# Fused windowed attention, Fourier mixing and a two-layer network on one core: more query and key buffers, a first load in three pieces, and PSUM banks lent to the first two batches

## The chip, the core and the metric

The kernel runs on one core of a Trainium2 chip. Its engines run side by side and are tied together by semaphores: TensorE (PE; its weight loads are shown apart as PEld), VectorE (DVE), ScalarE (ACT), GpSimd (POOL) and SyncE (SP). SP does nothing here but issue DMA transfers; ACT and POOL issue a few. The metric is the device time of one execution in microseconds, median of the runs.

## What is computed

All data is float32. Attention first: 8 batches, 8 heads, 576 positions, 64 columns a head. Heads 0 to 3 look at the last 32 positions, heads 4 to 7 at every fourth of the last 128. Its output, 576 rows of 512 a batch, goes through a Fourier mixing, a normalisation and two matrix products of 512 x 2048 and 2048 x 512:

```python
scores = np.where(masks, (q @ k.T) / sqrt(64), -1e9)
attn = exp(scores - max);  attn /= attn.sum() + 1e-9
x = (attn @ v)                       # (8, 576, 512)
u = x + real(fft(fft(x, axis=1), axis=2))
un = (u - mean(u)) / sqrt(var(u) + 1e-6)
out = u + relu(un @ w_ch1) @ w_ch2
```

## The kernel before

**A planner writes the order.** The program is not written in the order in which it runs. Each piece of work is given to a planner (`add`) with its engine, an estimated cost, the buffers it reads and writes, and a priority (the lower, the sooner). At build time the planner walks through an assumed clock: whenever an engine is free it takes the piece of lowest priority whose inputs are done and whose buffer has come free. A transfer is held back while eight of its queue are under way. The result is one fixed list for each engine, and on the chip each engine takes its list in order. `PAD_*` and `LAND` are lags added to the planner's costs, and the `P_*` constants are the priorities, in units of one attention step (twelve steps, 0 to 11, make a batch; batch b starts at 12 b).

**Attention.** A batch has four pairs of heads (`dil` 0 or 1, `j` 0 or 1). `attend_pair` loads a pair's keys into kb (L523, two transfers of 64 partitions), its queries into tq (L525) and its values into vt (L526), and calls `attend` three times (u = 0, 1, 2), each for two blocks of 96 queries. One such unit is: scores into a PSUM bank sc (L540), add the mask and take the maximum on VectorE into pm and mx (L548), exponential on ScalarE (L554), four transposes into bank pt (L567), a copy to ptsb on ScalarE (L570), the products with vt into bank av (L574), and on VectorE sums, reciprocal and the scaled result xt (L582 to L586). There are two tq buffers and three kb buffers. Keys are kept with zero halves around them, which `start` clears once with memsets (L478, L479). `store` writes xt to DRAM (xsp and xsm, L621).

**PSUM.** Eight banks in all: two each for sc, mix and ff, one each for pt and av.

**Mixing.** `mix` loads a batch's rows again (L693, L702; priority `P_FD` ahead of the work), folds them on POOL and VectorE, multiplies by the sequence and channel tables (L756, L802, banks mix), and normalises. The tables are loaded on POOL's queue by `table` (L499).

**Weights and fills.** The two weight matrices come as 64-bit numbers and are turned into float32 pairs by `words_of` and `halves` (L881 load, L882 on ScalarE, L884 to L893 and L900 on VectorE). `prep_w` does this for the first five of the sixteen blocks of 128 hidden columns, with priority `P_W + P_WF * f`; these stay on the core. `fill` computes the part of the two products that these five blocks give, 256 tokens at a time (L953 up, bank ff, L961 the split of h on VectorE, L969 down), with priority `P_FILL + 4 b P_FILLT` for batch b. There are 18 fills, and they need no more than the five blocks and the tokens, so the planner puts them where PE has room.

**The second half.** When all batches are mixed, the other eleven blocks are prepared, and nine chunks of 512 tokens run through them: five times `two_tiles`, once `one_tile`, with the down products of the tile before (`lower`) put between their up products (L1230). PE does almost nothing else from about 500 us on.

Of the kernel before, what the change touches and what calls it, by code (L numbers as in the profile page):

```python
# [19 lines left out]
P = 128  # L20
# [6 lines left out]
NX = 4  # L27
NKB = 3
NV = 4
NTQ = 2  # L30
NUT = 4
NUC = 2
NH = 6
NLATE = 4
NPE = 1
LO1 = 'DVE'
P_QK0, P_V0 = -7.8, -7.0
P_ST, P_FD, P_WD, P_ST0, P_FD0, P_SPAN0, P_SPAN1 = -4.0, -21.87, -10.91, 0.0, 0.0, 23.02, 23.31
P_QK, P_V, P_TR, P_MIX, P_SPAN, P_W, P_WF, P_FILL, P_FILLT = -8.0, -5.77, -5.0, 3.69, 13.04, 15.31, 8.7, 44.08, 3.7
P_MIX0, P_MIX1 = 3.0, 2.27  # L40
T_SEQ, T_CHN, T_STEP, P_SEQ, P_CHN = 7.07, 19.07, 0.08, -17.52, -2.0
PAD_PE, PAD_DVE, PAD_ACT, PAD_POOL, LAND = 0.0, 0.0, 0.0, 0.0, 1.5
XB = 1
P_MASK, P_ID, P_PERM = -7.19, -5.28, -7.0
NCH = B * S // TOK
# [336 lines left out]
def fused_kernel(ctx: ExitStack, tc, q, k, v, w1, w2, seq, tail, chn, alt, mask, ident, perm, flip, out):  # L382
# [76 lines left out]
    def dma(fn, r, w, prio, nbytes, slow=1):  # L459
        return add("SP", 0.46, fn, r, w, prio, nbytes * slow)  # L460
# [53 lines left out]
    def attend_pair(b, dil, j, xts, when):  # L514
        lead = when(0) + (P_QK if b else P_QK0)
        first = b == 0 and dil == 0 and j == 0
        tq = attw("tq", [P, S], F32, NTQ)
        kb = kbs[(4 * b + 2 * dil + j) % NKB]
        vt = attw("vt", [P, 2, S // QB, D + 1], F32, NV)
        on, eng = (nc.scalar, "ACT") if first else (nc.sync, "SP")  # L520
        for e in range(2):
            ps = slice(64 * e, 64 * e + 64)
            add(eng, 0.5, lambda e=e, ps=ps: on.dma_start(out=kb()[ps, e, WIN:], in_=k[b, dil, j, ps]),  # L523
                (), ((kb, e),), lead, 64 * S * 4)
        dma(lambda: nc.sync.dma_start(out=tq(), in_=q[b, dil, j]), (), (tq,), lead, P * S * 4)  # L525
        dma(lambda: nc.sync.dma_start(out=vt(), in_=v[b, dil, j]), (), (vt,), when(0) + (P_V if b else P_V0),  # L526
            P * 2 * (S // QB) * (D + 1) * 4)
        for u in range(3):
            attend(b, dil, j, u, tq, kb, vt, xts[u], when(u))

    def attend(b, dil, j, u, tq, kb, vt, xt, prio):
        blocks = (u, u + 3) if dil else (2 * u, 2 * u + 1)
        masks = DIL_MASK if dil else PLAIN_MASK
        sc = bank("sc")
        for n, t in enumerate(blocks):
            cols = slice(QB * t, QB * t + QB)
            keys = slice(QB * t, QB * t + KB)

            def scores(n=n, cols=cols, keys=keys):
                nc.tensor.matmul(  # L540
                    sc()[:QB, 256 * n:256 * n + 256], lhsT=tq()[:, cols], rhs=kb()[:, :, keys], start=True, stop=True,
                )
            add("PE", pe4(256), scores, (tq, kb), ((sc, n),), prio)
        pm = attw("pm", [QB, 4, KB], F32, 3)
# [8 lines left out]
        for i in range(4):  # L553
            add("ACT", 0.295, lambda i=i: nc.scalar.activation(  # L554
                out=pm()[:, i], in_=pm()[:, i], func=AF.Exp, bias=mx()[:, i:i + 1], scale=-1.0),
                ((mx, i),), ((pm, i),), prio)
        ps = bank("pt")
        for i in range(4):
# [12 lines left out]
            out=pt().rearrange("p i q -> p (i q)"), in_=ps()[:, :4 * QB]), (ps,), (pt,), prio)  # L571
        av = bank("av")
        for i in range(4):
# [716 lines left out]
    def one_tile(p, lower):  # L1290
        w = ups[p]
        z = bank("ff")
        product(z, 0, [(w[0], 0), (w[1], 1)], True, True, (z, 0))
        h1 = put_h(lambda: z()[:, 0:TOK1], ((z, 0),), False)
        lower(2)
        product(z, TOK1, [(w[2], 2), (w[0], 5)], True, True, (z, 1))
        h2 = put_h(lambda: z()[:, TOK1:TOK], ((z, 1),), False)
        lower(8)
        return [((h1, h2), downs[2 * p])]
# [46 lines left out]
```

## Time and profile before

| | us |
|---|---|
| median of 3 runs | 1099.94 (1099.26 to 1101.09) |
| the profiled execution, its own time | 1098.52 |
| its span in the trace | 1096.7 |
| PE busy | 1059.4 (97%) |
| VectorE busy | 742.9 (68%) |
| ScalarE busy | 520.9 (47%) |
| POOL busy | 283.1 (26%) |

The profiled execution's time is 1.8 us more than its span, which begins and ends with the core's own work. A busy PE is one that has matmuls under way, at whatever clock; the granted clock stands in a column of its own.

### The profile page before, as it was taken

The page shows a single profiled execution, that of the slowest core. Times are in us where ns is not written, and L with a number is a line of the kernel's source. Part 1 is how long each engine was busy: PE and PEld are TensorE (multiplying, and loading weights), DVE is VectorE, ACT ScalarE, POOL GpSimd, SP SyncE. Part 2 cuts the span into 40 slices and gives each one's busy share as a digit, 9 for nine tenths or more (in the row PEclk, how much of TensorE's full clock was granted, in tenths as well). Part 3 has the DMA queues.
Part 4 walks back from the last instruction along what each step waited for, and adds up shares of the span by engine and source line. Part 5 has one row for each costly group of instructions (what it writes and reads, how often), then busy time and mean ns, then how long its engine had stood idle before and what let it go on. Part 6 is the DMA issues. An engine that isn't in the chain of part 4 may idle for free.

```text
span 1096.7 us, 20233 instructions
## 1 busy us (share of the span) xinstructions
PE 1059.4 (97%) x7066; PEld 938.5 (86%) x7066; DVE 742.9 (68%) x2335; ACT 520.9 (47%) x1331; POOL 283.1 (26%) x334
## 2 busy tenths in 40 slices
PE   5889999999999998999999999999999999999998
PEld 4568889888888887899998988989899989898987
DVE  6689978878676759866899864637464555555432
ACT  4688845565465543424465434333333333333431
POOL 2023453544433415330000421212122130312200
PEclk9889999999999999999999999999999999999999
DMA  9687845756464533435634341404050505040211
GB/s 294 198 250 212 247 132 170 211 140 198 144 186 133 139 107 100 113 105 156 173 120 134 102 108 39 115 27 129 1 154 1 154 1 154 1 122 32 91 65 39
DMA packets 104310, 137.05 MB, mean 125 GB/s; under 512 B 9656, under 2 KB 62328, under 8 KB 104208
## 3 DMA queue, kind: packets, MB, share of 16 engines
q1 hardware_dynamic: 100624, 126.85, 41.0%
q0 software_dynamic: 3040, 8.09, 2.3%
q8 instruction: 56, 0.92, 0.4%
q10 hardware_dynamic: 544, 0.82, 0.2%
q14 instruction: 46, 0.38, 0.1%
HBM read 97.92 MB, written 37.80 MB: 124 GB/s over the span
## 4 chain that ended last, share of the span: by engine, by line
PE 80%; DVE 11%; DMA 3%; ACT 2%; issue 2%; SPq 1%; POOL 0%; ACTq 0%; DVEq 0%; POOLq 0%
PE sc L969 14%; PE ff L1230 12%; PE mix L1230 7%; PE sc L540 7%; PE ff L953 7%; PE ff L969 6%; PE av L969 5%; PE pt L969 5%; PE av L574 5%; PE mix L756 3%; PE mix L802 3%; PE pt L567 3%; PE pt L953 2%; DMA ut<-us 2%; DVE pm L548 2%
## 5 line engine op out<-in xcount | busy, mean ns | idle before, releaser
L554 ACT ACTIVATE pm<-pm,mx 96x128 f32<-96x128 f32 x384 | 129.6, 394 | 47.3 <-DVE mx L548 44.1
L540 PE MATMUL sc<-kb,tq 128*96 128x256 f32 x384 | 110.7, 405 | 10.9 <-DMA kb<-in_k_dram 6.9
L1246 ACT COPY s<-ff 128x256 f32<-128x256 f32 x135 | 50.1, 371 | 144.4 <-PE ff L1230 143.8
L548 DVE CUSTOM_DVE_ANT_0 pm<-sc,mask_sb 96x128 f32<-96x128 f32 x384 | 92.3, 280 | 31.5 <-PE sc L540 29.3
L953 PE MATMUL ff<-ut,wa 128*128 128x256 f32 x780 | 106.8, 287 | 4.2 <-DVE h L961 3.9
L969 PE MATMUL sc<-wa,h 128*128 128x512 f32 x420 | 104.4, 391 | 0.0
L953 PEld LDWEIGHTS ff<-ut,wa 128*128 128x128 f32 x780 | 97.1, 189 | 6.6 <-DVE h L961 4.7
L1098 POOL TENSOR_TENSOR ut<-ut 128x512 f32<-128x512 f32 x32 | 49.5, 1566 | 186.1 <-DVE ut L1051 185.5
L574 PEld LDWEIGHTS av<-vt,ptsb 128*96 128x96 f32 x768 | 77.1, 167 | 21.3 <-ACT ptsb L570 8.9
L969 PE MATMUL ff<-wa,h 128*128 128x512 f32 x390 | 93.9, 392 | 0.3 <-DVE r L645 0.3
L574 PE MATMUL av<-vt,ptsb 128*96 128x65 f32 x768 | 82.1, 249 | 8.8 <-ACT ptsb L570 4.4
L969 PEld LDWEIGHTS sc<-wa,h 128*128 128x128 f32 x420 | 76.0, 188 | 13.8
L1051 DVE STREAM_TRANSPOSE ut<-ut 128x512 f32<-128x512 f32 (+1 forms) x76 | 72.2, 982 | 18.7 <-DMA ut<-us 18.5
L969 PE MATMUL sc<-wd,h 128*128 128x512 f32 x324 | 84.1, 393 | 0.0
L969 PEld LDWEIGHTS ff<-wa,h 128*128 128x128 f32 x390 | 71.3, 188 | 14.4 <-DVE r L645 0.5
L1277 DVE TENSOR_TENSOR c<-s,s 128x256 f32<-128x256 f32 x45 | 26.7, 594 | 77.5 <-ACT s L1246 77.5
L1230 PEld LDWEIGHTS ff<-xb,pair 128*128 128x128 f32 x540 | 73.7, 188 | 6.0 <-ACT s L1246 0.3
L540 PEld LDWEIGHTS sc<-kb,tq 128*96 128x96 f32 x384 | 57.9, 173 | 24.0 <-issue 6.8
L1230 PE MATMUL ff<-xb,pair 128*128 128x256 f32 x540 | 76.4, 280 | 0.0
L1251 ACT ACTIVATE h<-row 128x256 fp32r<-128x256 f32 x90 | 37.6, 417 | 65.4 <-DVE row L1284 35.7
L1230 PE MATMUL mix<-xb,pair 128*128 128x256 f32 x486 | 65.1, 278 | 0.8 <-DVE row L1284 0.8
L969 PEld LDWEIGHTS sc<-wd,h 128*128 128x128 f32 x324 | 56.9, 188 | 9.6 <-DVE h L1253 0.3
(163 smaller groups left out, 2248.6 us busy)
## 6 DMA issues: line engine op xcount, KB each, us to landing
vt<-in_v_dram SPq DMA_DIRECT2D x32, 390.0 KB
ut<-in_w_dram SPq DMA_DIRECT2D x20, 512.0 KB
us<-uc SPq DMA_DIRECT2D x36, 257.0 KB
tq<-in_q_dram SPq DMA_DIRECT2D x32, 288.0 KB
part<-row SPq DMA_DIRECT2D x36, 256.0 KB
ut<-us SPq DMA_DIRECT2D x36, 256.0 KB
ut<-part SPq DMA_DIRECT2D x36, 256.0 KB
kb<-in_k_dram SPq DMA_DIRECT2D x62, 144.0 KB
```

The source lines that it names most:

```text
L540: nc.tensor.matmul(sc()[:QB, 256 * n:256 * n + 256], lhsT=tq()[:, cols], rhs=kb()[:, :, keys], start=True, stop=True,)
L548: nc.vector.tensor_tensor_reduce(pm()[:, i], sc()[:QB, KB * i:KB * i + KB], mask_sb()[:, masks[blocks[i // 2]]], -0.125, 3.0e38, ALU.add, ...
L554: add("ACT", 0.295, lambda i=i: nc.scalar.activation(out=pm()[:, i], in_=pm()[:, i], func=AF.Exp, bias=mx()[:, i:i + 1], scale=-1.0), ((mx ...
L567: nc.tensor.transpose(ps()[:, QB * i:QB * i + QB], pm()[:, i], order)
L574: add("PE", 0.17, lambda i=i: nc.tensor.matmul(av()[:QB, 65 * i:65 * i + 65], lhsT=pt()[:, i], rhs=vt()[:, i % 2, blocks[i // 2]], start=T ...
L953: nc.tensor.matmul(z()[:, :n_tok], lhsT=wf()[:, a, kk], rhs=ut()[:, p, kk], start=(kk == 0 and n == 0), stop=(kk == KT - 1 and n == 2),)
L969: nc.tensor.matmul(acc(), lhsT=h()[:, a, P * s:P * s + P], rhs=wf()[:, p], start=(first and n == 0), stop=(last and n == 2),)
L1051: nc.vector.transpose(out=o[back], in_=x[:, g])
L1098: add(name, cost(C), lambda: engine.tensor_tensor(out=made(i)(), in0=x(), in1=y(), op=ALU.subtract), (*done, *((raw, ("s", j)) for j in af ...
L1230: nc.tensor.matmul(z()[:, lo:lo + TOK1], lhsT=ap()[:, a, kk], rhs=xb()[:, j, p, kk], start=(start and k == 0), stop=(stop and k == 6 * len ...
L1246: add("ACT", act(TOK1), lambda: nc.scalar.copy(out=s(), in_=src()[:, :TOK1]), (src,), (s,), SOON - 1)
L1251: add("ACT", act(TOK1), lambda: nc.scalar.activation(out=h()[:, 0], in_=z(), func=AF.Relu), need, ((h, 0),), SOON)
```

## The change

A third tq buffer and a fourth kb buffer. The first pair's k and q are loaded in three pieces of 192 columns, one for each unit: of k only the first piece still goes out on ACT's queue, the rest on SP's, and each unit waits for its own pieces alone. In the first batch every second unit puts its transposes in a mix bank and its products in an ff bank instead of pt and av; in the second batch every second unit puts both in ff banks. `one_tile` takes two ff banks in place of two halves of one. The space reserved for the descriptors of POOL's transfers becomes 8192 bytes a partition. And the planner's priorities and lags get other values: among them, the weights of the first five blocks are due later (`P_W` from 15.31 to 30), fold loads less far ahead of their work (`P_FD` from -21.87 to -10.4), fills spread more (`P_FILLT` from 3.7 to 4.92), and ident_sb sooner (`P_ID`).

```diff
--- before.py
+++ after.py
@@ -25,23 +25,24 @@
 TOK = 4 * P
 TOK1 = 2 * P
 NX = 4
-NKB = 3
+NKB = 4
 NV = 4
-NTQ = 2
+NTQ = 3
 NUT = 4
 NUC = 2
 NH = 6
 NLATE = 4
+NOPEN = 2
 NPE = 1
 LO1 = 'DVE'
 P_QK0, P_V0 = -7.8, -7.0
-P_ST, P_FD, P_WD, P_ST0, P_FD0, P_SPAN0, P_SPAN1 = -4.0, -21.87, -10.91, 0.0, 0.0, 23.02, 23.31
-P_QK, P_V, P_TR, P_MIX, P_SPAN, P_W, P_WF, P_FILL, P_FILLT = -8.0, -5.77, -5.0, 3.69, 13.04, 15.31, 8.7, 44.08, 3.7
-P_MIX0, P_MIX1 = 3.0, 2.27
-T_SEQ, T_CHN, T_STEP, P_SEQ, P_CHN = 7.07, 19.07, 0.08, -17.52, -2.0
-PAD_PE, PAD_DVE, PAD_ACT, PAD_POOL, LAND = 0.0, 0.0, 0.0, 0.0, 1.5
+P_ST, P_FD, P_WD, P_ST0, P_FD0, P_SPAN0, P_SPAN1 = -4.0, -10.4, -10.91, -3.44, -4.94, 29.11, 21.73
+P_QK, P_V, P_TR, P_MIX, P_SPAN, P_W, P_WF, P_FILL, P_FILLT = -8.0, -5.91, -5.0, -1.75, 9.95, 30, 8.7, 42.98, 4.92
+P_MIX0, P_MIX1 = 4.1, 2.27
+T_SEQ, T_CHN, T_STEP, P_SEQ, P_CHN = 7.07, 23.47, 0.08, -5.61, -2.0
+PAD_PE, PAD_DVE, PAD_ACT, PAD_POOL, LAND = 0.0, 0.2, 0.1, 0.2, 1.5
 XB = 1
-P_MASK, P_ID, P_PERM = -7.19, -5.28, -7.0
+P_MASK, P_ID, P_PERM = -7.35, -7.37, -7.0
 NCH = B * S // TOK
 NREST = 4 * B
 NTILE = B * S // P
@@ -517,18 +518,32 @@
         tq = attw("tq", [P, S], F32, NTQ)
         kb = kbs[(4 * b + 2 * dil + j) % NKB]
         vt = attw("vt", [P, 2, S // QB, D + 1], F32, NV)
-        on, eng = (nc.scalar, "ACT") if first else (nc.sync, "SP")
-        for e in range(2):
-            ps = slice(64 * e, 64 * e + 64)
-            add(eng, 0.5, lambda e=e, ps=ps: on.dma_start(out=kb()[ps, e, WIN:], in_=k[b, dil, j, ps]),
-                (), ((kb, e),), lead, 64 * S * 4)
-        dma(lambda: nc.sync.dma_start(out=tq(), in_=q[b, dil, j]), (), (tq,), lead, P * S * 4)
+        cuts = [slice(192 * x, 192 * x + 192) for x in range(3)] if first else [slice(0, S)]
+        for x, cs in enumerate(cuts):
+            n = cs.stop - cs.start
+            on, eng = (nc.scalar, "ACT") if first and x == 0 else (nc.sync, "SP")
+            for e in range(2):
+                ps = slice(64 * e, 64 * e + 64)
+                add(eng, 0.5, lambda e=e, ps=ps, cs=cs, on=on: on.dma_start(
+                    out=kb()[ps, e, WIN + cs.start:WIN + cs.stop], in_=k[b, dil, j, ps, cs]),
+                    (), ((kb, (e, x) if first else e),), lead + 0.3 * x, 64 * n * 4)
+            dma(lambda cs=cs: nc.sync.dma_start(out=tq()[:, cs], in_=q[b, dil, j, :, cs]),
+                (), ((tq, x),), lead + 0.3 * x, P * n * 4)
         dma(lambda: nc.sync.dma_start(out=vt(), in_=v[b, dil, j]), (), (vt,), when(0) + (P_V if b else P_V0),
             P * 2 * (S // QB) * (D + 1) * 4)
         for u in range(3):
-            attend(b, dil, j, u, tq, kb, vt, xts[u], when(u))
-
-    def attend(b, dil, j, u, tq, kb, vt, xt, prio):
+            if first:
+                kneed = tuple((kb, (e, x)) for e in range(2) for x in range(u + 1)) + ((kb, ("z", 0)), (kb, ("z", 1)))
+                attend(b, dil, j, u, ((tq, u),), kneed, vt, xts[u], when(u), tq, kb)
+            else:
+                attend(b, dil, j, u, (tq,), (kb,), vt, xts[u], when(u), tq, kb)
+
+    def seat(b, n, own):
+        if b >= NOPEN or n % 2 == 0:
+            return own
+        return "mix" if own == "pt" and b == 0 else "ff"
+
+    def attend(b, dil, j, u, qneed, kneed, vt, xt, prio, tq, kb):
         blocks = (u, u + 3) if dil else (2 * u, 2 * u + 1)
         masks = DIL_MASK if dil else PLAIN_MASK
         sc = bank("sc")
@@ -540,7 +555,7 @@
                 nc.tensor.matmul(
                     sc()[:QB, 256 * n:256 * n + 256], lhsT=tq()[:, cols], rhs=kb()[:, :, keys], start=True, stop=True,
                 )
-            add("PE", pe4(256), scores, (tq, kb), ((sc, n),), prio)
+            add("PE", pe4(256), scores, (*qneed, *kneed), ((sc, n),), prio)
         pm = attw("pm", [QB, 4, KB], F32, 3)
         mx = attw("mx", [QB, 4], F32, 3)
         for i in range(4):
@@ -554,7 +569,7 @@
             add("ACT", 0.295, lambda i=i: nc.scalar.activation(
                 out=pm()[:, i], in_=pm()[:, i], func=AF.Exp, bias=mx()[:, i:i + 1], scale=-1.0),
                 ((mx, i),), ((pm, i),), prio)
-        ps = bank("pt")
+        ps = bank(seat(b, 6 * dil + 3 * j + u, "pt"))
         for i in range(4):
             def turn(i=i):
                 t = blocks[i // 2]
@@ -569,7 +584,7 @@
         pt = attw("ptsb", [P, 4, QB], F32, 3)
         add("ACT", act(4 * QB) - 0.05, lambda: nc.scalar.copy(
             out=pt().rearrange("p i q -> p (i q)"), in_=ps()[:, :4 * QB]), (ps,), (pt,), prio)
-        av = bank("av")
+        av = bank(seat(b, 6 * dil + 3 * j + u, "av"))
         for i in range(4):
             add("PE", 0.17, lambda i=i: nc.tensor.matmul(
                 av()[:QB, 65 * i:65 * i + 65], lhsT=pt()[:, i],
@@ -1289,12 +1304,12 @@
 
     def one_tile(p, lower):
         w = ups[p]
-        z = bank("ff")
-        product(z, 0, [(w[0], 0), (w[1], 1)], True, True, (z, 0))
-        h1 = put_h(lambda: z()[:, 0:TOK1], ((z, 0),), False)
+        z, y = bank("ff"), bank("ff")
+        product(z, 0, [(w[0], 0), (w[1], 1)], True, True, z)
+        h1 = put_h(lambda: z()[:, 0:TOK1], (z,), False)
         lower(2)
-        product(z, TOK1, [(w[2], 2), (w[0], 5)], True, True, (z, 1))
-        h2 = put_h(lambda: z()[:, TOK1:TOK], ((z, 1),), False)
+        product(y, 0, [(w[2], 2), (w[0], 5)], True, True, y)
+        h2 = put_h(lambda: y()[:, 0:TOK1], (y,), False)
         lower(8)
         return [((h1, h2), downs[2 * p])]
 
@@ -1331,7 +1346,7 @@
         q=columns(inputs["q"]), k=columns(inputs["k"]), v=windows(inputs["v"]),
         w1=inputs["moe_w_ch1"].view(np.int64), w2=inputs["moe_w_ch2"].view(np.int64), **tables()
     )
-    nc = _bacc.Bacc("TRN2", target_bir_lowering=False, num_devices=1)
+    nc = _bacc.Bacc("TRN2", target_bir_lowering=False, num_devices=1, dynamic_dma_scratch_size=8192)
     arrays, args = {}, []
     for name, a in arrays_in.items():
         a = np.ascontiguousarray(a)
```

## Rows read from the trace of the kernel before

**Rows 1.** The page, part 1: busy us of each engine, share of the span, and number of instructions.

```profile
PE 1059.4 (97%) x7066; PEld 938.5 (86%) x7066; DVE 742.9 (68%) x2335; ACT 520.9 (47%) x1331; POOL 283.1 (26%) x334
```

**Rows 2.** Table of wide stretches, whole core. Columns: us of the stretch A:B, its length, then busy us (and instructions) of PE, PEld (weight loads), DVE (VectorE), ACT (ScalarE) and POOL (GpSimd), the granted TensorE clock as a share of full speed, the mean busy share of the DMA engines, and GB/s.

```profile
0.00:50.00 50.00, 34.47 (x208) 25.51 (x208) 32.02 (x188) 26.25 (x72) 5.72 (x14) 0.86 0.86 253
0.00:150.00 150.00, 129.36 (x934) 106.72 (x934) 124.22 (x648) 103.35 (x284) 41.93 (x63) 0.93 0.76 225
40.00:60.00 20.00, 17.33 (x125) 13.25 (x126) 14.83 (x92) 15.48 (x45) 0.00 (x0) 1.00 0.69 207
80.00:150.00 70.00, 68.75 (x561) 61.73 (x560) 66.08 (x325) 53.07 (x147) 29.93 (x41) 1.00 0.68 202
150.00:500.00 350.00, 340.27 (x2407) 301.01 (x2407) 263.71 (x1033) 177.32 (x472) 140.78 (x196) 1.00 0.52 148
420.00:460.00 40.00, 36.12 (x230) 31.82 (x230) 38.12 (x74) 18.60 (x44) 16.69 (x20) 1.00 0.49 134
500.00:1080.00 580.00, 578.30 (x3669) 521.22 (x3668) 350.86 (x647) 239.38 (x574) 100.42 (x76) 1.00 0.32 87
1080.00:1097.00 17.00, 11.44 (x62) 9.57 (x61) 4.07 (x7) 0.85 (x3) 0.00 (x0) 0.97 0.22 63
```

**Rows 3.** Table of fine stretches at the start, columns as in rows 2.

```profile
4.00:31.00 27.00, 17.79 (x105) 12.94 (x106) 18.55 (x102) 13.13 (x38) 5.54 (x10) 0.87 1.13 324
12.33:18.60 6.27, 5.89 (x48) 4.77 (x49) 4.47 (x29) 5.15 (x16) 0.00 (x0) 1.00 1.16 340
19.00:34.00 15.00, 9.25 (x48) 6.20 (x48) 11.13 (x52) 7.71 (x21) 2.65 (x5) 0.67 1.02 325
25.00:37.00 12.00, 9.40 (x31) 6.19 (x32) 8.47 (x35) 5.66 (x17) 0.00 (x0) 0.50 0.74 239
63.00:72.00 9.00, 6.33 (x39) 4.54 (x39) 8.72 (x34) 6.43 (x16) 2.01 (x2) 0.80 0.67 197
...
69.00:75.00 6.00, 5.28 (x21) 3.79 (x20) 4.83 (x26) 3.92 (x11) 1.90 (x3) 0.50 0.78 236
```

**Rows 4.** Waits of PE over the whole span: who waited for whom, us in total, times, longest.

```profile
PE sc L540 <- DMA kb<-in_k_dram: 6.9, 1, 6.9
```

**Rows 5.** PE in order of time: start, us, engine, line, operation, out<-in, shapes, how many; in brackets the idle time before it and what ended it.

```profile
6.87 3.69 PE L540 MATMUL sc<-kb,tq 128*96 128x256 f32 x8 [6.87 <-DMA kb<-in_k_dram]
...
10.73 1.03 PE L540 MATMUL sc<-kb,tq 128*96 128x256 f32 x4
12.33 0.89 PE L574 MATMUL av<-vt,ptsb 128*96 128x65 f32 x8 [0.57 <-ACT ptsb L570]
...
17.74 1.03 PE L540 MATMUL sc<-kb,tq 128*96 128x256 f32 x4
18.60 0.81 PE L574 MATMUL av<-vt,ptsb 128*96 128x65 f32 x8
...
25.24 2.88 PE L540 MATMUL sc<-kb,tq 128*96 128x256 f32 x6 [1.54 <-DMA tq<-in_q_dram]
30.11 0.71 PE L567 MATMUL pt<-perm_sb,pm 96*128 96x96 f32 x2 [2.00 <-ACT pm L554]
...
75.91 1.06 PE L756 MATMUL mix<-seq,ees 128*128 128x290 f32 x6
...
113.97 0.70 PE L953 MATMUL ff<-ut,wa 128*128 128x256 f32 x3
```

**Rows 6.** Waits of SP's queue in the first 130 us, columns as in rows 4. L525 is the load of tq.

```profile
SPq L525 <- PE sc L540: 23.1, 10, 8.0
```

**Rows 7.** SP's queue in order of time: when a load was issued and how long the issue took.

```profile
9.67 1.27 SPq L881 DMA_DIRECT2D ut<-in_w_dram  x2
...
12.48 0.35 SPq L525 DMA_DIRECT2D tq<-in_q_dram  x1
```

**Rows 8.** VectorE in order of time, columns as in rows 5: a memset of a key buffer, three operations of a weight preparation (L884, L887, L900), the first mask operation of the third pair, and two operations of the second dip.

```profile
5.48 0.56 DVE L478 MEMSET kb<- 64x608 f32 x1
...
27.07 0.42 DVE L884 TENSOR_SCALAR ut<-ut 128x512 uint32<-128x512 uint32 x1
...
27.52 0.69 DVE L887 SCALAR_TENSOR_TENSOR ut<-ut 128x512 uint32<-128x512 uint32 x1
28.13 0.68 DVE L900 TENSOR_TENSOR wa<-ut,wa 128x512 fp32r<-128x512 f32 x1
...
29.33 0.28 DVE L548 CUSTOM_DVE_ANT_0 pm<-sc,mask_sb 96x128 f32<-96x128 f32 x1
...
65.62 1.11 DVE L887 SCALAR_TENSOR_TENSOR ut<-ut 128x512 uint32<-128x512 uint32 x1
66.65 0.41 DVE L586 TENSOR_TENSOR xt<-av,rinv 96x256 f32<-96x256 f32 x1
```

**Rows 9.** DMA engines from 0 to 60 us: GB/s in 40 slices of 1.5 us.

```profile
GB/s 0 172 263 234 359 215 315 279 249 295 394 389 364 394 408 242 308 389 370 331 377 297 21 0 38 267 229 321 370 169 0 136 220 10 187 196 266 247 276 286
```

**Rows 10.** Waits of PE from 40 to 150 us, columns as in rows 4.

```profile
PE av L574 <- DVE xt L586: 2.1, 5, 1.0
PE pt L567 <- ACT ptsb L570: 1.2, 2, 0.6
```

**Rows 11.** PE in order of time, one whole fill near the end of the first half, columns as in rows 5.

```profile
470.35 7.23 PE L953 MATMUL ff<-ut,wa 128*128 128x256 f32 x60
477.41 7.01 PE L969 MATMUL ff<-wa,h 128*128 128x512 f32 x30
```

## The prediction

> **What bounds the kernel now.** I read the page's busy shares first: TensorE is busy for 1059.4 of the 1096.7 us span [rows 1]. The number of matmuls doesn't change, so only two things can be won or lost: the 37.3 us in which PE stands idle, and work done at the lower clock. The table of wide stretches shows where the idle time is [rows 2]: 20.6 us before 150 us (15.5 of them before 50), 9.7 between 150 and 500, 1.7 in the 580 us to 1080, and 5.6 at the end, where the last results drain. So the early stretch decides, and I cut it finer [rows 3]: from 19 to 34 us PE idles 5.75 us, and from 25 to 37 us the granted clock is 0.50, the lower of its two levels (1.2 GHz). A second dip has 2.67 us idle between 63 and 72 and a clock of 0.50 from 69 to 75.
>
> The waits and the order of work name the causes. The first scores wait 6.9 us for the transfer of kb [rows 4], those at 25.24 for that of tq [rows 5]. SP's queue says why: it stood 23.1 us in ten waits where a tq load waits for score matmuls that still read the old buffer [rows 6]. With two tq buffers the third pair's tq can't be issued before the first pair's scores are done; it goes out at 12.48, behind the loads of vt and two 512 KB weight rows [rows 7]. The DMA engines are full from 4 to 31 us (share 1.13 [rows 3]), so it lands just before 25.24. What is late next is VectorE: while PE was empty it began on weight preparation, so the scores of 25.24 get their first pm at 29.33 only [rows 8], and the next transposes come at 30.11 [rows 5]. The second dip is VectorE's as well: it is busy for 8.7 of the 9 us from 63 to 72 [rows 3], with weight preparation (L887, 1.11 us) ahead of the xt at 66.65 [rows 8], for which PE's single av bank waits.
>
> **The change part by part.** The profiled execution took 1098.5 us, 1.4 below the median shown; the sum is made from 1098.5.
>
> *First pair in three pieces.* The first unit's scores now need a third of kb and tq (98 KB of each) instead of 295 KB. The kb rows landed by 6.87; the DMA engines move nothing in the first 1.5 us [rows 9], so kb took the 5.4 us after that, beside the others. A third of it, by the same share and with about 1 us left for latency (an estimate), lands near 4. But SP now issues seven transfers for this pair instead of one. Six more, at about 0.45 us (0.35 for a tq, 0.64 for a weight row [rows 7]), are 2.7 us before the first vt, and four of the seven go before mask_sb. Bytes up to and with mask_sb: 4 x 98 + 197 (ident_sb) + 147 = 737 KB; the slices of [rows 9] add up to that a little before 5 us, so with 1 us of latency pm starts near 6.2 instead of 8.9, which the first unit's av follows at its old distance: near 9.6 instead of 12.33 [rows 5]. vt is the eleventh issue, near 5.7, and 1.45 MB end with it, which the slices pass at 7.3: just in time. I take 2.5 us; the bounds are 0 (vt late by all six issues) and 3.5.
>
> *Three tq, four kb.* The third pair's tq, some 3.1 to 4.7 MB down the queues (three pairs of k and q, two or three vt, the tables), lands between 14 and 18 us by [rows 9], before 18.77 us, where the last scores that PE has are done [rows 5]. Attention then goes on at the pace of before: from 12.33 to 18.60, three units, PE is busy for 5.89 of 6.27 us [rows 3]. Take a tenth idle instead: 1.5 of 15 us against 5.75. Gain 4.2, bounds 0 and 5.7. The extra kb costs two large memsets of 0.56 us [rows 8] and two small ones, 1.3 us of VectorE before its first pm; should the other early work not leave room, pm comes 1.3 us later, which lies within the 0 above.
>
> *The clock.* PE was busy for 9.4 us at 0.50 between 25 and 37 [rows 3]: 4.7 us of work at the upper level. With the gap before it gone I take 4.5; bounds 0 and 5.3 (the partly slow edges too).
>
> *Weight preparation later* (P_W from 15.31 to 30). One preparation costs VectorE 0.42 + 3 x 0.69 + 0.68 = 3.2 us [rows 8]. Out of the second dip it gives back up to 2.67 us of idle and half of the 5.28 us busy at 0.50 [rows 3]: 5.3 in all. I take 3 (bounds 0 and 5.3), since fold and xt stay there. The work doesn't vanish. VectorE was busy for 124.2 of the first 150 us, and for 66.1 of the last 70 of them, 94% [rows 2]; if all of it must still be done at that rate, after 8 us of start, it takes until 140: a gain of at most 10. What exceeds that must move behind 150, where VectorE is at 75% [rows 2], and the fills that need these weights go with it. I charge 2.5 us; bounds 0 and 6.
>
> *Lent banks.* pt and av have one bank each. PE idles 2.67 us in 40 to 60 [rows 2], mostly in short waits of av for xt and of pt for ptsb [rows 10]. With every second unit in another bank these overlap: I take 1, bounds 0 and 2.5. The lenders stand empty: the first mix matmul is at 75.91, the first ff matmul at 113.97 [rows 5], about the ends of the batches that borrow.
>
> *No cost, no gain.* The second ff bank in one_tile: PE idles 1.7 us in 580 there [rows 2], so no wait is left to remove, and the other ff bank was freed before eight down products. The smaller descriptor space touches POOL's loads alone; POOL is busy for 283 of 1097 us [rows 1], and should a table load wait for space, the first mix matmul at 75.91 leaves some 50 us for it. Fills that fall due later (step 3.70 to 4.92) reorder 150 to 500; idle there is 9.7 us now, I take 0, bounds -5 and +5.
>
> Sum: 2.5 + 4.2 + 4.5 + 3 + 1 - 2.5 = 12.7. 1098.5 - 12.7 = 1085.8, with the 1.4 of the median 1087.2. I say 1087.
>
> **The rivals.**
> (a) *Only part comes.* VectorE binds at once. Attention alone takes 4.47 of 6.27 us of it [rows 3], so each preparation of 3.2 us needs five units to hide in, and ten of them more than the first two batches have. Then the second dip stays (3 lost), the banks give nothing (1), the clock half (2.2): 6.5 are left, 1093.5. For it: 94% busy from 80 us on. Against: VectorE idles 18 of the first 50 us [rows 2].
> (b) *The clock stays low.* The first eight score matmuls took 3.69 us from 6.87, four of them 1.03 later [rows 5]: PE starts slow and speeds up after work. Units that arrive piece by piece leave gaps; if the slow time runs on to 12 us and the dip at 25 only moves, start and clock are lost, 7 us: 1094. The Trainium skill, "TensorE: Matmul & The Clock Gate", Part 1, has it that the throttled state is the default and activity lifts it; by that rule the earlier scores would be slow ones. The trace agrees in direction (3.69 against 1.03 us) and can't show it for the new start.
> (c) *No change.* The DMA engines are full, so an earlier tq displaces something that is needed as soon. Then 1098 to 1102. Against: what it displaces is weight rows, first used at 113.97.
> (d) *Slower.* Fills due later pile up after the attention with nothing beside them. Between 420 and 460 us fills ran nearly alone, and PE idled 3.9 of 40 us [rows 2], a tenth, in waits for VectorE's h. A fill is 60 matmuls in 7.23 us and 30 in 7.01 [rows 11], 14.2 us, so each one pushed into such a stretch costs 1.4 us, and 1.7 at worst. Ten of the 18 would cost 15 and give 1102 or more; it decides from nine on. For it: fills of a batch now fall due 19.7 after those of the last one, against 12 for attention. Against: the planner still takes a fill whenever PE has nothing more urgent.
>
> **How the numbers follow.** Chances: the sum 0.58 (its own range 1080 to 1093), (a) 0.12, (b) 0.10, (c) 0.06, (d) 0.14. About 0.2%, 2.2 us, is what a measurement of this kernel can tell from no change. Faster is the first three, 0.80; same 0.06; slower 0.14. The range leaves out (d) and a little of (c); below, it ends where every gain is at its upper bound without the charge (3.5 + 5.7 + 5.3 + 5.3 + 2.5 = 22.3, so 1077.6): 1078 to 1100.
>
> **What would show it.** First scores near 4 us and first av near 9.6; no gap of over 1 us between 19 and 31, and full clock there; SP's waits of tq loads for scores far below 23 us; no weight preparation on VectorE in the second batch; still 1.7 us of idle after 500. I am wrong if PE's idle time before 150 us stays near 20, or if that between 150 and 500 grows by as much as the start gains.

## The result and the profile after

The changed kernel takes 1074.99 us (1073.34 to 1077.08 in 4 runs), against 1099.88 for the one before on the same chip: a ratio of 0.9773 (0.9753 to 0.9793), 25 us less. The direction was the predicted one, the size twice the forecast, and the time lies below the range. The profiled execution took 1075.66, its span is 1073.9.

The page's busy shares come first, to be held against [rows 1]:

```profile
PE 1048.4 (98%) x7066; PEld 936.4 (87%) x7066; DVE 747.0 (70%) x2339; ACT 514.6 (48%) x1331; POOL 286.8 (27%) x334
```

PE's idle time fell from 37.3 us to 25.5 (1073.9 - 1048.4). That is 11.8 of the 22.8 us by which the span shrank. The other 11.0 came out of time that both pages count as busy. Some 4.9 of them are the clock: PE was busy for 16.2 us at 0.50 before and for 6.4 after, and half of that time is lost. The table of wide stretches (columns as in [rows 2]) shows the places:

```profile
0.00:50.00 50.00, 41.51 (x280) 31.80 (x280) 34.17 (x242) 32.92 (x98) 5.72 (x14) 1.00 0.94 262
...
100.00:150.00 50.00, 42.41 (x300) 34.24 (x299) 47.70 (x239) 38.20 (x103) 14.24 (x18) 0.93 0.84 235
150.00:500.00 350.00, 346.83 (x2504) 316.08 (x2504) 278.81 (x987) 172.59 (x458) 150.38 (x202) 1.00 0.51 146
500.00:1060.00 560.00, 559.37 (x3550) 504.79 (x3549) 337.28 (x613) 228.65 (x551) 99.30 (x76) 1.00 0.31 84
```

In the first 50 us PE gains 7.0 us of busy time, at full clock (34.47 before). In 150 to 500 it gains 6.6 (340.27 before). Between 100 and 150 the share is poor: 42.41 of 50.

The fine stretches, as in [rows 3], show both early stalls gone: 19 to 34 us now has 14.78 busy of 15, and the clock, 0.50 before in 25 to 37 and in 69 to 75, is 1.00.

```profile
19.00:34.00 15.00, 14.78 (x117) 12.08 (x118) 10.48 (x85) 12.76 (x40) 2.66 (x5) 1.00 1.16 308
25.00:37.00 12.00, 11.00 (x78) 8.15 (x76) 8.31 (x67) 10.37 (x33) 2.40 (x5) 1.00 1.08 296
63.00:72.00 9.00, 8.98 (x64) 7.42 (x62) 8.20 (x48) 8.17 (x26) 2.73 (x4) 1.00 0.93 286
69.00:75.00 6.00, 6.00 (x52) 5.35 (x51) 5.90 (x25) 6.00 (x21) 0.00 (x0) 1.00 0.99 280
```

PE in order of time, to be read beside [rows 5]: the first scores start at 4.03 instead of 6.87, but the first av at 12.32, as before. The second unit's av is in the lent ff bank, the third's in av again. The longest wait for a tq up to 50 us is 0.46.

```profile
4.03 3.70 PE L555 MATMUL sc<-kb,tq 128*96 128x256 f32 x8 [4.03 <-DMA kb<-in_k_dram]
...
12.32 1.01 PE L589 MATMUL av<-vt,ptsb 128*96 128x65 f32 x8
...
14.23 0.81 PE L589 MATMUL ff<-vt,ptsb 128*96 128x65 f32 x8
14.88 0.84 PE L589 MATMUL av<-vt,ptsb 128*96 128x65 f32 x8
...
19.15 0.64 PE L555 MATMUL sc<-kb,tq 128*96 128x256 f32 x2 [0.46 <-DMA tq<-in_q_dram]
```

SP's queue in the first 130 us ([rows 6]) no longer has 23.1 us of tq loads behind scores; one such wait of 0.5 us is left. Its longest waits are now stores of xt (L636; 9.8 us before, 18.2 now), and the largest of a tq load (L530) is for a transfer of vt:

```profile
SPq L636 <- DVE mx L563: 18.2, 12, 5.3
...
SPq L530 <- DMA vt<-in_v_dram: 2.0, 1, 2.0
```

**An account that needs no idle time.** Idle time and clock give 16.7 of the 22.8 us, so I count otherwise. From the traces I took what each kind of matmul costs at full clock when matmuls follow one another: the 60 of [rows 11] begin at 470.35 and the next run at 477.41, so one costs 0.118 us, though the view gives the run 7.23 us. The other kinds likewise: 0.228 for 512 columns, 0.2175 for scores, 0.0825 for a transpose, 0.081 for av, the rest by their columns. All 7066 make 1024.0 us of work. Time lost by t is then t less the work started by t. It holds idle time, low clock, and the 0.17 us at the end of a run that counts as busy even when nothing follows. The number of matmuls is the same in all kernels, so at the end an error in a unit cost falls on all of them alike. At an earlier time the kernels have started different kinds, and another reasonable set of unit costs moves the entries by up to 1 us.

```
us lost by          25    50    75   100   150   300   500   end
before            13.9  24.9  34.5  36.6  39.7  47.8  62.8  72.7
after             10.6  15.7  17.7  19.0  34.0  37.5  42.8  49.9
before + lags     13.5  25.8  30.4  32.5  34.3  40.0  47.8  53.7
after - lags      11.3  17.4  20.1  21.3  39.2  48.9  57.2  71.3
buffers + lags    10.6  21.9  31.7  33.5  38.2  43.0  50.2  56.2
weights early     10.5  19.8  28.1  31.2  39.4  48.2  54.9  62.1
first pair whole  10.4  18.4  20.6  22.2  38.1  42.4  47.0  56.1
nothing lent      11.2  21.5  22.6  23.5  39.7  46.8  50.8  58.5
memsets later     14.8  21.6  24.4  26.0  40.8  46.0  50.0  57.6
```

After is 17.6 us ahead at 100 us, has 5.7 of it left at 150, wins 14.3 between 150 and 500 and 2.8 behind that. The rows below the second are experiments, named in the next section.

### The profile page after: what moved, and what is told of

Its sections match the earlier page's. It is cut to its first block, busy times and chain, and to the rows that moved or that the text cites. A ratio compares the mean times of both kernels' runs of the same rounds, so it can differ in the third digit from the quotient of the medians.

```text
span 1073.9 us, 20225 instructions
## 1 busy us (share of the span) xinstructions
PE 1048.4 (98%) x7066; PEld 936.4 (87%) x7066; DVE 747.0 (70%) x2339; ACT 514.6 (48%) x1331; POOL 286.8 (27%) x334
## 4 chain that ended last, share of the span: by engine, by line
PE 82%; DVE 11%; DMA 4%; ACT 1%; SPq 1%; issue 1%; DVEq 0%; ACTq 0%
PE sc L984 15%; PE ff L1245 14%; PE mix L1245 8%; PE ff L968 7%; PE ff L984 6%; PE pt L984 6%; PE av L984 6%; PE sc L555 4%; PE av L589 4%; PE mix L817 3%; PE mix L771 2%; PE pt L968 2%; DVE pm L563 2%; PE pt L582 2%; PE av L968 1%; DMA xsm<-xt 1%
## 5 line engine op out<-in xcount | busy, mean ns | idle before, releaser
L555 PE MATMUL sc<-kb,tq 128*96 128x256 f32 x384 | 106.5, 396 | 6.4 <-DMA kb<-in_k_dram 4.0
L589 PEld LDWEIGHTS av<-vt,ptsb 128*96 128x96 f32 x672 | 67.9, 167 | 13.9 <-issue 5.0
L589 PE MATMUL av<-vt,ptsb 128*96 128x65 f32 x672 | 71.9, 249 | 6.3 <-DVE xt L601 4.5
L1022 POOL DMA_INDIRECT ut<-us,flip_sb x20 | 19.8, 989 | 176.3 <-DMA ut<-us 84.7
L1126 POOL TENSOR_TENSOR xb<-ut,xb 128x512 fp32r<-128x512 f32 x24 | 31.0, 1295 | 131.2 <-ACT xb L1123 131.2
```

Source lines behind the costliest of these rows:

```text
L555: nc.tensor.matmul(sc()[:QB, 256 * n:256 * n + 256], lhsT=tq()[:, cols], rhs=kb()[:, :, keys], start=True, stop=True,)
L589: add("PE", 0.17, lambda i=i: nc.tensor.matmul(av()[:QB, 65 * i:65 * i + 65], lhsT=pt()[:, i], rhs=vt()[:, i % 2, blocks[i // 2]], start=T ...
```

## The experiments

Changes against the kernel before are given as (ratio - 1) x 1100 us, with the 95% interval of the ratio, so that runs on different chips stand on one scale.

**First: both halves alone.** The structure (buffers, pieces, lent banks) with every old priority and lag, and the new priorities and lags on the old structure.

```diff
 after.py                                  # e1_structure
-P_W ... = 30 ...;  PAD_DVE, PAD_ACT, PAD_POOL = 0.2, 0.1, 0.2
+P_W ... = 15.31 ...;  PAD_DVE, PAD_ACT, PAD_POOL = 0.0, 0.0, 0.0
 before.py                                 # e2_order: the reverse
```

> The changed kernel with all the old priorities and lags; buffers, pieces, lent banks and the two ff banks stay. Counted as time minus the matmul work done at full clock, the changed kernel is 17.6 us ahead of the old one at 100 us, has 5.7 left at 150, wins 14.3 more from 150 to 500 and 2.8 after that. Theory 1 (the structure wins the early part, the new order the late part): 100 us is still won by some 15 us, little is given back at 150 because the weights are prepared as early as before, and nothing is won from 150 to 500: 1082 to 1088. Theory 2 (the structure is worth nothing without the new order, since the old one interleaves weight preparation with the units): 1093 to 1100. Theory 3 (the structure is all of it): 1073 to 1078.

> The old kernel with all the new priorities and lags, two tq and three kb buffers, whole first loads, no lent banks. Theory 1: the stall on tq near 25 us and the low clock after it stay, the gain from 150 to 500 comes (10 to 14 us), minus the weights' late block: 1086 to 1094. Theory 2 (order is nearly all): 1076 to 1082. Theory 3 (order is nothing): 1097 to 1103.

The structure alone brings nothing: 1.0012 (0.9993 to 1.0032). The new order alone, which includes the lags, brings 13.8 us: 0.9875 (0.9846 to 0.9903). In the structure alone PE's av waits three times in the first 100 us for the xt of the unit before, 4.9 us together (2.0 in five waits before; PE in order of time, of the structure with old priorities):

```profile
41.92 1.42 PE L589 MATMUL av<-vt,ptsb 128*96 128x65 f32 x8 [1.30 <-DVE xt L601]
...
47.67 1.52 PE L589 MATMUL av<-vt,ptsb 128*96 128x65 f32 x8 [1.77 <-DVE xt L601]
...
73.01 1.54 PE L589 MATMUL av<-vt,ptsb 128*96 128x65 f32 x8 [1.84 <-DVE xt L601]
```

**Then one part taken back from after at a time.**

```diff
-NKB = 4                                   # e3_buffers
-NTQ = 3
+NKB = 3
+NTQ = 2
-NOPEN = 2                                 # e4_nolent
+NOPEN = 0
-P_W = 30                                  # e5_weights
+P_W = 15.31
-P_FILL, P_FILLT = 42.98, 4.92             # e6_fills
+P_FILL, P_FILLT = 44.08, 3.7
-PAD_DVE, PAD_ACT, PAD_POOL = 0.2, 0.1, 0.2    # e7_lags
+PAD_DVE, PAD_ACT, PAD_POOL = 0.0, 0.0, 0.0
-P_ST0 = -3.44                             # e8_stores
+P_ST0 = 0.0
-first = b == 0 and dil == 0 and j == 0    # e11_whole
+first = False
```

> The changed kernel with two tq and three kb buffers, all else as changed. Theory 1: SP waits some 20 us again for scores before it may load tq, the third pair's scores start near 22 to 25 us, and 5 to 9 us are lost, with the low clock: 1080 to 1085. Rival (the stall was the order of the loads on the queue, weights ahead of tq, which the priorities mend): 1074 to 1077.

> The changed kernel without lent banks, all else as changed. By the prediction's term they are worth 1 us (bounds 0 and 2.5): 1074 to 1078. Rival (they are what lets two units run at once: with them the av products came in pairs and 12 more units were done by 66 us than the old pace allows): 1080 to 1088, with the loss before 80 us.

> The changed kernel with P_W at 15.31 again, all else as changed. Theory 1 (the late weights make the early part, and cost the stretch from 100 to 150): the lead at 100 us falls by 3 to 8, the stretch from 100 to 150 loses some 10 less, the end 1074 to 1081. Rival (late weights only pay back what they win, 12 us between 100 and 150): faster than the changed kernel, 1066 to 1072.

> The changed kernel with P_FILL and P_FILLT as before (44.08, 3.70). The changed one loses 8.8 us between 150 and 500, the old one 23.1. If the spread fills bring that: 10 or more of the 14 us are lost again there, 1084 to 1090. If they don't: 1073 to 1077, and the late gain is the lags' or the mix's.

> The changed kernel with the lags of the planner at 0 again (PAD_DVE 0.2, PAD_ACT 0.1, PAD_POOL 0.2 in the changed one). If the lags bring the gain between 150 and 500 (work placed later than its inputs by a margin, so that the engine whose list is in order rarely stands behind a late one): 5 to 14 us lost, most of it between 150 and 500, 1080 to 1089. If not: 1073 to 1077.

> The changed kernel with P_ST0 at 0 again (priority of the first batch's stores of xt; -3.44 in the changed one). With old priorities and the new structure the xt of the third pair waited until 41.45 for its buffer, whose store stood on SP's queue behind the loads. If that is what kept the structure from paying: the lead at 50 us falls by 4 to 8, and 1079 to 1084. If other priorities did: 1073 to 1077.

> The changed kernel with the first pair's k and q loaded whole. The prediction gave the pieces 2.5 us; in the changed trace the first scores start 2.84 us sooner, but the first av is at 12.32 as before, and three av products are done by 15.7 instead of two. Theory (the pieces win a unit at most, since pm still starts at 8.55): 1074 to 1077, a loss of 0 to 2. Rival (the term was right): 1077 to 1079.

```
taken back from after      ratio to before            change
(nothing: after)           0.9773 (0.9753 to 0.9793)  -25.0
lags            e7         0.9942 (0.9921 to 0.9964)   -6.4
weights later   e5         0.9888 (0.9860 to 0.9917)  -12.3
pieces          e11        0.9861 (0.9842 to 0.9880)  -15.3
lent banks      e4         0.9848 (0.9831 to 0.9866)  -16.7
fills           e6         0.9812 (0.9780 to 0.9843)  -20.7
stores          e8         0.9767 (0.9740 to 0.9794)  -25.6
```

Taking back the lags costs 18.6 us, the most. For the fills the interval overlaps with that of after. Of these expectations only e4 (its rival) and e8 held one range that came true; e5, e6, e7 and e11 came out between or beyond theirs. The five that cost something cost 53.6 us together (e3 and its mended form come below): they aren't shares of the gain. Each hands the planner another problem, and the list changes. In the kernel without lags the table of wide stretches shows where:

```profile
0.00:50.00 50.00, 42.45 (x280) 32.91 (x281) 33.54 (x230) 31.16 (x90) 5.74 (x14) 1.00 0.93 261
...
150.00:500.00 350.00, 343.29 (x2457) 307.82 (x2458) 281.66 (x992) 172.90 (x456) 146.27 (x202) 1.00 0.51 146
500.00:1060.00 560.00, 556.15 (x3510) 500.83 (x3510) 332.71 (x602) 227.20 (x543) 100.35 (x76) 1.00 0.32 86
```

Its start is as good as after's (42.45 busy against 41.51 by 50 us), but 150 to 500 idles 6.7 us against 3.2, and 500 to 1060 3.85 against 0.6.

**The lags alone, on the kernel before.** This was the run that decided. With it went the structure with old priorities and new lags.

```diff
 before.py                                 # e9_lags_alone; after.py with old priorities: e10
-PAD_DVE, PAD_ACT, PAD_POOL = 0.0, 0.0, 0.0
+PAD_DVE, PAD_ACT, PAD_POOL = 0.2, 0.1, 0.2
```

> The old kernel with nothing changed but the planner's lags (0.2, 0.1, 0.2 us on what VectorE, ScalarE and POOL hand on). Taking them out of the changed kernel cost 20 us. Theory 4 (the lags by themselves keep PE from standing behind late inputs, whatever the plan): 1084 to 1091, and the loss between 150 and 500 falls from 23.1 to 15 or less. Rival (they only fit with the new priorities, which were chosen with them): 1096 to 1103.

> The changed kernel with the old priorities but the new lags: buffers, pieces, lent banks and lags, no new due times. With lags 0 as well it took 1102. Theory 4: 1080 to 1090. Rival (the late weights carry the early part; putting them back alone cost 13): 1090 to 1100.

One line of the old kernel gives 1078.81 us, 0.9796 (0.9775 to 0.9816): 22.4 of the 25, and more than Theory 4 had allowed. Its table of stretches:

```profile
0.00:50.00 50.00, 34.45 (x203) 26.20 (x204) 33.67 (x188) 26.20 (x71) 5.72 (x14) 0.86 0.85 253
25.00:37.00 12.00, 8.60 (x32) 5.71 (x31) 8.94 (x38) 6.12 (x16) 0.00 (x0) 0.65 0.81 258
63.00:72.00 9.00, 8.24 (x68) 6.96 (x69) 7.54 (x42) 6.72 (x19) 3.71 (x6) 1.00 0.89 251
69.00:75.00 6.00, 5.22 (x40) 4.39 (x40) 5.20 (x32) 4.92 (x15) 2.43 (x5) 1.00 0.90 271
150.00:500.00 350.00, 345.54 (x2479) 310.95 (x2478) 270.56 (x1047) 182.23 (x485) 141.18 (x193) 1.00 0.53 154
500.00:1060.00 560.00, 560.00 (x3564) 506.11 (x3563) 334.52 (x617) 230.97 (x554) 100.87 (x76) 1.00 0.31 85
```

The early stall and its clock are still there (33.67 of VectorE and 34.45 of PE by 50 us, 0.65 granted in 25 to 37), as two tq buffers leave them. But the second dip is gone: 8.24 busy of 9 in 63 to 72 and a clock of 1.00, where [rows 3] had 6.33 and then 0.50, and the weights are as early as before (five of the ten preparations done by 75 us in both). 150 to 500 idles 4.5 us instead of 9.7. PE's waits in that stretch, first the three largest of eight in the kernel before, then with the lags alone:

```profile
PE ff L953 <- DVE h L961: 3.9, 4, 1.4
PE sc L540 <- DVE mx L548: 1.5, 5, 0.4
PE pt L567 <- ACT pm L554: 1.5, 4, 0.9
...
```

```profile
PE ff L953 <- DVE h L961: 2.7, 3, 1.6
PE sc L540 <- DVE mx L548: 0.8, 1, 0.8
PE ff L969 <- DVE h L961: 0.2, 1, 0.2
```

With the lags alone these three are all that the view has left. The waits of transposes for pm (1.5 us in 4) are gone, those of scores for mx are one instead of five, and all waits add up to 3.7 us instead of 9.1. In the code a lag makes the planner reckon a result ready 0.2 us later for the other engines (0.1 for ScalarE's), and its buffers free as much later; where it has another matmul to put between, it does.

That view counts only waits that leave a gap. With the unit costs I can also count matmuls that began 0.02 us or more late behind a signal of VectorE or ScalarE, gap or not, from 150 to 500:

```
                     matmuls   us late   VectorE   ScalarE
before                    51      16.2      10.6       5.6
before + lags             32       8.3       7.0       1.3
after                     18       5.5       5.0       0.5
after - lags              40      11.9      10.3       1.6
```

Of the 16.2 us before only 9.5 show as gaps. The lags alone take away 7.9 of them, at the hand-overs of both engines.

The structure with lags and old priorities is at 0.9876 (0.9853 to 0.9899), 8.8 us worse than the lags without the structure. So neither the structure (e10) nor the new due times (e2) add to the lags by themselves. Each takes away from them, and both together are 2.5 us better, which overlapping intervals don't tell from nothing.

**Is it the lags, or another draw of the plan?** A change of a constant can give another list. A nudge of `P_FILL` redraws it, from about 110 us on, with no other content; half and double lags give a size.

```diff
-P_FILL = 44.08                            # e13_redraw, before.py; e14: with the lags
+P_FILL = 43.9
+PAD_DVE, PAD_ACT, PAD_POOL = 0.1, 0.05, 0.1    # e15_half, before.py
+PAD_DVE, PAD_ACT, PAD_POOL = 0.4, 0.2, 0.4     # e16_double, before.py
```

> The old kernel with P_FILL at 43.9 instead of 44.08, lags 0: the same work, due times moved by nothing that matters, but the planner's choice between equals falls otherwise from about 110 us on, so the lists differ. It measures how far the time moves when the plan is only drawn again. If the 21 us of the lags alone are a lucky draw: this one too moves by 5 or more either way. If they are the lags' own: 1096 to 1104.

> The old kernel with the new lags and P_FILL at 43.9: the second draw with lags. Lags' own: 1074 to 1084. A lucky draw: 1085 or more.

> The old kernel with half the lags (0.1, 0.05, 0.1). If the gain grows with the margin: between 1083 and 1095. If any margin does: 1075 to 1082. If only this one value does (a draw): 1095 to 1103.

> The old kernel with double the lags (0.4, 0.2, 0.4). If more margin is better still: 1070 to 1077. If the margin is as large as the lateness it covers: 1076 to 1084. If too large a margin puts work needlessly late: 1084 to 1095.

The redraw moves nothing, 0.9994 (0.9978 to 1.0009), and with the lags it gains 20.6 us, 0.9813 (0.9785 to 0.9840). Half the lags gain 7.8, 0.9929 (0.9909 to 0.9948), double 19.0, 0.9827 (0.9801 to 0.9853). So, by two draws and three sizes, it is the lags' own effect; it grows up to the size chosen, and doubling that adds nothing. In all four surroundings in which I switched them (e9 against before, e14 against e13, e10 against e1, after against e7) they are worth 22.4, 19.9, 15.0 and 18.6 us.

**The buffers.** Alone on the old structure with the lags; and, mended, taken back from after.

```diff
 before.py + lags                          # e17_buffers_alone
-NKB, NTQ = 3, 2
+NKB, NTQ = 4, 3
 after.py, NKB = 3, NTQ = 2                # e18_buffers_mended
-kneed = ... + ((kb, ("z", 0)), (kb, ("z", 1)))
+kneed = ... + ((kb, ("z", 0)), (kb, ("z", 1)), (kb, 0), (kb, 1))
```

> The old kernel with the new lags and with three tq and four kb buffers, nothing else; beside the old kernel with the lags alone (1078.8, ratio 0.9796), in which the third pair's first transposes still come at 30.02 and 25.8 us are lost by 50. The prediction gave the removed stall and the clock behind it 8.7 us: 1068 to 1073 by it. Rival (what is won before 40 us is given back, as VectorE has the same work to do and the weights' preparation then stands in the way): no gap over 1 us between 19 and 31 and 4 to 8 us less lost by 40, but 1076 to 1083.

> The changed kernel with two tq and three kb buffers once more, now with the first pair's reads tied to the buffer's next load. In e3_buffers they were not: the fourth pair's keys were loaded over the first pair's before these were read, so a part of the first scores used wrong keys, and its early stretch tells nothing of the buffers. If the buffers are worth what the prediction said (8.7 us, with the rest of the change in place): 1081 to 1087. If more, because the lent banks and the late weights build on them: 1087 to 1095. If nothing: 1073 to 1078.

The mended kernel takes 0.9830 (0.9807 to 0.9852): the buffers cost 6.3 us when taken back from after. The kernel of e3 (0.9946) loaded keys over others that were still to be read, so its time says nothing of the buffers. Added to the lags alone they bring nothing: 0.9838 (0.9818 to 0.9859) against 0.9796. (That run also has the 8192-byte descriptor space of the changed kernel, which the text ahead of it doesn't say; the space alone was not tried.) Yet the stall goes as I said. Of the lags and buffers, the table of stretches:

```profile
19.00:31.00 12.00, 9.50 (x75) 7.12 (x74) 6.98 (x55) 8.57 (x26) 2.65 (x5) 1.00 1.20 357
25.00:37.00 12.00, 8.61 (x51) 5.82 (x52) 7.92 (x49) 8.66 (x25) 0.00 (x0) 1.00 1.10 331
...
38.00:48.00 10.00, 8.93 (x46) 7.23 (x46) 6.83 (x31) 4.92 (x13) 0.00 (x0) 0.50 0.47 128
...
63.00:72.00 9.00, 8.38 (x39) 6.99 (x39) 6.49 (x33) 5.47 (x18) 2.79 (x4) 0.50 0.63 177
69.00:75.00 6.00, 6.00 (x39) 5.22 (x39) 3.79 (x26) 3.93 (x14) 3.12 (x5) 0.74 0.99 292
```

From 19 to 31 no gap is over 0.79 us, though PE is busy for only 9.50 of 12 us, not for nine tenths as I took it, and 25 to 37 runs at full clock. But the low clock has mostly moved: 38 to 48 is at 0.50, with PE busy for 8.93 us, so some 4.5 us are lost there. At 50 us this kernel has lost 21.9 us, 3.9 less than with the lags alone. By 75 it is 31.7 against 30.4: a second dip to 0.50 has opened at 63 to 72.

**The memsets at the start.** In after VectorE clears four key buffers with two large memsets each, 0.56 us a memset, before its first pm; this is the last of the eight:

```profile
7.79 0.56 DVE L479 MEMSET kb<- 64x608 f32 x1 [0.17 <-issue]
...
8.55 0.29 DVE L563 CUSTOM_DVE_ANT_0 pm<-sc,mask_sb 96x128 f32<-96x128 f32 x1
```

```diff
-zero(t, "DVE", 0.8, clear, ("z", e), -6.0 + n)          # e12_memsets
+zero(t, "DVE", 0.8, clear, ("z", e), 3.0, at=11.0)      # third and fourth kb; eot and ye too
```

> The changed kernel with the memsets of the third and fourth key buffer, eot and ye held back to 11 us of the planner's clock, behind the first unit's pm. In the changed kernel VectorE clears buffers without a break from 5.48 to 8.43 and starts pm at 8.55, though the first scores were done near 6. Theory (memsets hold the first unit back): first pm near 6.5, first av near 10.5, 1072 to 1074. Rival (mask_sb, issued at 3.61, lands no sooner than 8): first pm near 8.3, 1074 to 1077.

The first pm comes at 6.18, the first av at 10.96 instead of 12.32 (VectorE, then PE, in order of time):

```profile
6.18 0.29 DVE L563 CUSTOM_DVE_ANT_0 pm<-sc,mask_sb 96x128 f32<-96x128 f32 x1 [2.18 <-PE sc L555]
```

```profile
10.96 0.86 PE L589 MATMUL av<-vt,ptsb 128*96 128x65 f32 x8 [0.45 <-DMA vt<-in_v_dram]
...
14.84 1.94 PE L555 MATMUL sc<-kb,tq 128*96 128x256 f32 x8 [2.00 <-DMA tq<-in_q_dram]
```

But av then waits for vt, a later score run waits 2.00 us for its tq, and the kernel is slower than after: 0.9832 (0.9800 to 0.9864). Memsets were what was late, and with them gone the transfers are. Why the whole kernel ends 6.5 us behind after isn't shown by these waits alone.

## Why the prediction was wrong

Two steps failed: the lags got no term at all, and the term for 150 to 500 us was put at nothing. The count that all of it rested on was also too small.

**"Only two things can be won or lost"** was that count: 37.3 us of idle time, and the work at the lower clock, which costs some 8 us after the start. The account gives 72.7 us lost. Of 22.8 us won, 11.8 were visible as idle and 4.9 as clock; some 6 were neither. PE counts as busy to the end of a run, so a hand-over that is a little late shows no idle time, or 0.17 us less of it than it costs. This alone wouldn't have put the time out of the range; the next two did.

**The lags had no term.** I read them as padding in a cost table and priced buffers and priorities instead. Alone they are 22.4 us (e9). They weren't in the sum, nor among the rivals, nor in what would make the prediction wrong.

**"Fills that fall due later ... I take 0, bounds -5 and +5"** is the term in which the miss shows. The loss in 150 to 500 fell from 23.1 us to 8.8, 14.3 less, and behind 500 by another 2.8. I had bounded it by 9.7 us of idle time with room for half; visible idle time there fell by 6.6, the rest didn't show. The lags alone give 9.6 of the 14.3 and 4.0 behind 500. Nor did the range use the term's own bound: its lower end adds up the early gains and leaves these 5 us out. With them it would have ended near 1073, and 1075 would have lain inside, though for a reason that I didn't have. PE's waits in this stretch of after add up to 2.9 us, the longest of them for h (3.9 us in four waits before):

```profile
PE ff L968 <- DVE h L976: 1.5, 1, 1.5
...
PE sc L555 <- DVE mx L563: 0.3, 1, 0.3
...
```

**The early terms were right in sum, in part by luck.** Pieces, buffers, clock, weights and banks made 15.2 us; at 100 us after has lost 17.6 less. The stall and both dips went as said. Two of the terms are not as I had them:
- The pieces: scores came near 4 us as forecast, the first av at 12.32 and not near 9.6. I let 1.3 us of memsets vanish within a bound; the last of eight ends at 8.35, and pm starts at 8.55. The 1 us of latency that I used came from no row: the scores kept to it, but vt, which I had landed at 7.3, held up av until 10.96 once the memsets were out of the way (e12). At 25 us the kernel with the first pair whole has lost no more than after (10.4 against 10.6). Why it ends 9.7 us later isn't shown.
- The second dip I gave to weight preparation ahead of xt, and that is what stands there: in after, taking the weights back to 15.31 opens a hole, 1.89 us busy of 6, with scores waiting 3.20 us for a mask operation that comes behind preparations and xt. But the weights needn't go: the lags alone close the dip with as many preparations done by 75 us. It is a matter of where the list puts them. (Of after with the weights early: stretches, then VectorE and PE in order of time.)

```profile
69.00:75.00 6.00, 1.89 (x11) 1.41 (x12) 5.65 (x19) 3.10 (x8) 3.48 (x3) 0.82 0.83 271
100.00:150.00 50.00, 47.46 (x336) 41.52 (x335) 43.27 (x190) 30.67 (x84) 20.94 (x27) 0.93 0.67 188
```

```profile
69.51 1.05 DVE L915 TENSOR_TENSOR wa<-ut,wa 128x512 fp32r<-128x512 f32 x1
...
70.88 0.42 DVE L601 TENSOR_TENSOR xt<-ff,rinv 96x256 f32<-96x256 f32 x1
```

```profile
74.00 1.17 PE L555 MATMUL sc<-kb,tq 128*96 128x256 f32 x2 [3.20 <-DVE mx L563]
```

**"I charge 2.5; bounds 0 and 6" measured 11.9.** Between 100 and 150 us after loses 15.0 us and before 3.1. My rate for VectorE was right (47.70 us busy of 50), but I concluded that the gain could reach 10 by 140 us; it was 5.7 at 150. The groups of PE's instructions in 100 to 150 show what that means, of after and then of before:

```profile
L555 PE MATMUL sc<-kb,tq 128*96 128x256 f32 x68 | 19.7, 412 | 1.3 <-DVE mx L563 1.3
L589 PE MATMUL av<-vt,ptsb 128*96 128x65 f32 x128 | 14.6, 260 | 4.8 <-DVE xt L601 3.7 <-issue 1.0
...
L968 PE MATMUL ff<-ut,wa 128*128 128x256 f32 x18 | 2.4, 286 | 0.0
...
L817 PE MATMUL mix<-chn,y 128*128 128x258 f32 x1 | 0.3, 282 | 0.0
```

```profile
L574 PE MATMUL av<-vt,ptsb 128*96 128x65 f32 x139 | 14.6, 246 | 0.5 <-DVE xt L586 0.3
L540 PE MATMUL sc<-kb,tq 128*96 128x256 f32 x52 | 13.9, 383 | 0.1
L953 PE MATMUL ff<-ut,wa 128*128 128x256 f32 x60 | 10.6, 303 | 0.0
L802 PE MATMUL mix<-chn,y 128*128 128x258 f32 (+1 forms) x37 | 6.0, 290 | 0.2 <-ACT pc L812 0.2
```

VectorE is as full in both (47.46 before, by the same table). Before, PE had 60 up matmuls of fills and 37 of the channel mix to do beside the attention; after has 18 and 1, since the weights come late: two of ten preparations are done by 100 us (seven before), and its first fill starts at 146.5, before's at 114.0. With little but attention, PE waits for xt, and its clock falls to 0.93. With the weights early (e5) it has 60 and 21 again and is busy for 47.46 us. So part of the work that I called "moved behind 150" was the cover for VectorE's wait. Only part: by the account that kernel still loses 8.2 us here, at the same clock of 0.93, so the late weights give about 7 of the 11.9 and the rest stays open. Nor is `P_W` alone what makes the weights late: in the new order on the old structure seven preparations are done by 100 us, as before.

**Rivals.** None happened. Of (b), the start was as slow as it said (3.70 us for the first eight), but the slow time didn't run on, and 25 to 37 was at 1.00; the dip that only moves came in the kernel with buffers and lags (38 to 48). (d) came nearest the place and had the wrong sign: fills due later did not pile up; 150 to 500 is where the time was won. What decided it was the lags, which the rival did not weigh.

**What stays open.** Whether one engine's lag would do (DVE's alone, say) wasn't tried, nor were the remaining new priorities (`P_FD`, `P_MIX` and others) one by one. Nor is it shown why the parts taken back from after cost 4 to 13 us each; that each redraws the plan is argued only, for the redraw that I measured, on the old kernel, moved nothing. No run beats after beyond its interval: old store priorities (e8) give 0.9767 against 0.9773.

## What to carry to other kernels

In a program whose order is fixed ahead by a planner, give every hand-over between engines slack in the planner's own model and measure its size first: here one line by itself was worth 22 us of 1100, nine tenths of what a change with a dozen parts gave. Bound what can be won by elapsed time less the work at full rate, not by the idle time of the busiest engine. When a stall's cause is removed, look for the work that filled the next stretch: early gains of 17.6 us were down to 5.7 fifty microseconds later, in part because what was put off had been cover.

## What the runs showed of the hardware

A run of 60 matmuls shows 7.23 us of busy time where 7.06 pass to the start of the next, so a run's end can hide up to 0.17 us. With a PE at 97%, 72.7 of 1096.7 us were lost against work at full clock, and 37.3 of them showed as idle. The granted clock fell with a gap of 2.67 us in 9 before (to 0.50 from 69 to 75), and stayed at 1.00 with 0.76 us of gaps in the same 9 us in the kernel with the lags alone. The first eight score matmuls took 3.70 us from 4.03 as they had taken 3.69 from 6.87: an earlier start was an equally slow one.
